# Block-causal attention and experts in one kernel: in the late turns, the scores of pair n on both sides of the sums of values of pair n-1

## The chip, the cores and the metric

The kernel runs on one core of a Trainium2 chip. The metric is the device time of one execution in microseconds (us); 1096.31 us is the median of three runs before the change. The engines named below are the tensor engine (PE, matmuls), the vector engine (DVE), the scalar engine (ACT), GpSimd (POOL) and the queue engine (SP). Each works through its own instructions in the order in which they were written into the program; semaphores tie the engines together. Matmuls write into PSUM, which the kernel uses as eight banks of 128 x 512 float32 (the tags `w0` to `w3`, `acc0` to `acc2` and `h`).

## The reference

Attention over 8 batches and 8 heads, 576 positions of 64 dimensions, masked in blocks of 64, and then two matmuls with a gate over all 4608 rows:

```python
scores = q @ k.T / 8                       # per batch and head, 576 x 576
mask = (pos[:, None] // 64) >= (pos[None, :] // 64)
attn = softmax(where(mask, scores, -1e9))
x = attn @ v                               # heads side by side: 4608 x 512
h = x @ w_in                               # 512 -> 2048
out = (h / (1 + exp(-1.702 * h))) @ w_out  # 2048 -> 512
```

All is float32. The kernel gets near-float32 products by splitting operands into a high and a low part (`high`, `low`; `xh`, `xl`; `wih`, `wil`; `gh`, `gl`) and adding three products.

## The kernel before

Two heads make a pair; there are 32 pairs, n = 0 to 31, and the program has 33 turns, one a pair and a last one for what is left over. Turns 0 to 7 are early turns, in which the weights of the experts are unpacked beside the attention. From turn 8 on the experts' matmuls run between the pieces of attention; turns 9 to 31 are the late turns of which this document speaks. Each turn is a row of slots (`ORDER`, `START`, `HANDOVER`, `FIRST_LATE`); after each slot `advance` writes as much of the experts' work as a schedule asks for. In turns from 9 on it always stops right behind the `hp` matmuls of a chunk (`state["gate"]`), so attention on PE always follows an `hp` matmul.

**Attention of a pair.** The 576 queries of a pair are cut into five rows: row 0 has 64 queries, rows 1 to 4 have 128, and row i needs 64(2i+1) keys, so 64, 192, 320, 448 and 576. For each row and head:

- scores: three matmuls on PE into a bank (`score_into`, from `high` and `low`);
- the score operation on DVE: mask, scale and running minimum of the bank in one instruction, with a small read-out instruction behind it (`weigh`, L439);
- exp with its sum on ACT (L446);
- normalising (`normalise`): two small instructions on DVE and a multiplication, on POOL for rows 0 to 3 and on DVE for row 4;
- transposes of the weights on DVE into `tw` (`turn`, L474 and L479), after which 16 DMAs on SP's queue bring them to `pw`; both are parts of the tile `turned`;
- the sums of values (`av`): 60 matmul instructions on PE from `pw` and the values `vp` into two banks, o0 and o, which ACT then copies to `xr` (L557, L558).

Before that, `prep_late` transposes q and k of a pair on DVE (L323), casts them to `high` on ACT (L324) and makes `low` on POOL.

**Banks.** In the experts' time three banks (w0, w1, w2) go round for attention, one more is lent by the experts (`lent_bank`: the spare one of two that hold `hp`), and the others hold `acc` and `hp`. The sums of a late turn take 320 columns of o0 and 256 of o. Row 4 has 576 keys and does not fit a bank: its first 384 go to two other banks, its last 192 lie beside the sums, in o0 for the first head and in o for the second (`beside` in `av`).

**A late turn before.** Slot 0 scores rows 3, 0, 2 and 1 of pair n in four banks, one stretch on PE. N and T normalise and transpose them. Slot V (`av(n-1)`) sums the values of pair n-1 and then scores row 4 of pair n; behind it come the preparation of pair n+1 (`prep`), row 4's normalising and transposing, and the DMAs to `pw`.

**Experts.** A tile is 384 rows. Per tile there are 16 chunks: 12 `hp` matmuls of 384 columns, then the gate: tanh on ACT (L673), a product on DVE (L674, tile g), a cast to `gh` on ACT (L682), the rest `gl` on POOL (L88). The nine `acc` matmuls of 512 columns of a chunk follow one chunk later. The gate's instructions have a high priority, by which a scheduler sets them among DVE's and ACT's other work; PE's matmuls keep the order of the code.

Of the kernel before, what the change touches and what calls it, by code (L numbers as in the profile page):

```python
# [25 lines left out]
ORDER = (  # L26
# [3 lines left out]
)  # L30
# [11 lines left out]
def attention_moe_kernel(  # L42
# [33 lines left out]
    def early(n):  # L76

        return n < 2 * HP
# [270 lines left out]
    def prep(n):  # L349

        if not parts_of(n):
            qk[n] = room("e0" if n % 2 else "qk", [P, 2, S], F32, "qk")
            for x in range(2):
                nc.vector.transpose(out=qk[n][:, x], in_=raw[n][:, x].rearrange("p c d -> p (c d)"))
        else:
            prep_late(n)
        raw.pop(n)
        m = follower(n)
        if m is not None:
            load(m)  # L360

    stats = {}
# [1 line left out]
    def score(n, banks):  # L364

        turns["late"] = not early(n)
        if n not in stats:
            mx = d2.tile([P, NCH + 1, 2], F32, tag="mx", name="mx")
            sm = d2.tile([P, NCH, 2], F32, tag="sm", name="sm")
            stats[n] = (mx, sm)  # L370
        todo = []
        taken = 0
        for chunks in banks:

            part = []
            for lo, hi in ((0, 512),) if width(chunks[0]) <= 512 else ((0, 256), (256, S)):
                ss = []
                for _ in range(2):
                    taken += 1
                    ss.append(lent_bank() if taken == 1 and turns["late"] else bank())  # L380
                c = 0
                for i in chunks:
                    a, z = qrange(i)
                    w = min(hi, width(i)) - lo
                    score_into(n, a, [x[:, c : c + w] for x in ss], lo, lo + w)
                    part += [(i, hd, lo, lo + w, ss[hd][0 : z - a, c : c + w]) for hd in range(2)]
                    c += w
            todo.append(sorted(part, key=lambda x: (chunks[::-1].index(x[0]), x[2])))
        settle(n, banks, todo)

    def settle(n, banks, todo):
        for chunks, part in zip(banks, todo):
            e = {}
            for i, hd, lo, hi, s in part:
                if i not in e:
                    e[i] = es[i] if early(n) else weights_of(n, i)
                weigh(n, i, hd, lo, hi, s, e[i])
            if early(n):
                for i in chunks[::-1]:
                    if n == 2 * HP - 1 and i == NCH - 1:  # L400
                        with tc.high_priority(offset=300):
                            normalise(n, i, e[i])
                    else:
                        normalise(n, i, e[i])
            else:
                weighed.extend((n, i, e[i]) for i in chunks[::-1])
            if 4 in chunks and not early(n):
                if n + 1 < NPAIR and n != 2 * HP:
                    prep(n + 1)
                normalise_all()  # L410
                turn_all()

    weighed = []
    shared = {}

    def weights_of(n, i):
        if i > 2:
# [5 lines left out]
    def normalise_all():  # L423
        for x in weighed:
            normalise(*x)

    def turn_all():
        for x in weighed:
            turn(*x)
        weighed.clear()  # L430

    def weigh(n, i, hd, lo, hi, s, e):
# [6 lines left out]
        nc.vector.tensor_tensor_reduce(  # L439
            out=e[0:m, hd, lo:hi], in0=s, in1=mk,  # L440
            op0=ALU.add, op1=ALU.min, scale=-0.125,
            scalar=3e38 if lo == 0 else mx[0:m, NCH, hd : hd + 1],
            accum_out=mx[0:m, i, hd : hd + 1] if hi == w else mx[0:m, NCH, hd : hd + 1],
        )
        if hi == w:
            nc.scalar.activation(  # L446
                out=e[0:m, hd], in_=e[0:m, hd], func=AF.Exp, scale=-1.0,
                bias=mx[0:m, i, hd : hd + 1], accum_out=sm[0:m, i, hd : hd + 1],
            )

    def normalise(n, i, e):
# [6 lines left out]
        if not early(n) and i == NCH - 1:  # L458
# [12 lines left out]
    def turn(n, i, e):  # L471

        for hd in range(2 if i else 0):
            nc.vector.transpose(  # L474
                out=tw[:, :, SLOT[i] : SLOT[i] + i, hd].rearrange("p b j c -> p j b c"),
                in_=e[:, hd, 0 : i * P],
            )
        r = slice(BLK, P) if i else slice(0, BLK)
        nc.vector.transpose(  # L479
            out=tw[r, 0:2, 9 + max(i, 1)].rearrange("p b h c -> p h b c"), in_=e[r, :, i * P : width(i)]  # L480
        )
        if i == NCH - 1:
            for kb in range(4):
                for qb in range(4):
                    ns = 10 if kb > 1 else NS if qb > 1 else 11
                    nc.sync.dma_start(
                        out=pw[kb * 32 : kb * 32 + 32, qb, 0:ns], in_=tw[qb * 32 : qb * 32 + 32, kb, 0:ns]
                    )

    def flip(n, chunks):  # L490

# [23 lines left out]
                in_=src[:, x : x + 2 * len(part), a : a + 2],  # L515
            )

    def av(n):

        b, h = divmod(n, HP)  # L520
        before_av(n)
        if turns["late"]:
            o0, o = bank(), bank()
            cut = BLK + 2 * P
        else:
            o, o0 = bank(), bank()
            cut = BLK

        def place(q0):
            return (o0, q0) if q0 < cut else (o, q0 - cut)  # L530

        todo = []
        for i in range(1, NCH):
# [3 lines left out]
        todo.append((*place(0), BLK, 0, pw[:, 0:2, 10]))  # L537

        ends = [[x for x, y in enumerate(todo) if y[0] is bk] for bk in (o0, o)]
        for x, (bk, c, nn, j, w) in enumerate(todo):  # L540
            for hd in range(2):
                mm(
                    out=bk[hd * D : hd * D + D, c : c + nn].rearrange("d (a c) -> d a c", c=32),
                    lhsT=values(n)[:, hd, j], rhs=w[:, :, hd],
                    start=any(x == y[0] for y in ends), stop=any(x == y[-1] for y in ends),
                )
        m = n + 1
        rest = []
        if turns["late"] and m < NPAIR:
# [6 lines left out]
        c0 = (b % 2) * S  # L556
        nc.scalar.copy(out=xr[:, h, c0 : c0 + cut], in_=o0[:, 0:cut])  # L557
        nc.scalar.copy(out=xr[:, h, c0 + cut : c0 + S], in_=o[:, 0 : S - cut])  # L558
        nxt = follower(n)
        if nxt is not None:  # L560
            load_v(nxt)
        if rest:
            settle(m, [[4]], [sorted(rest, key=lambda x: x[2])])

    def follower(n):

# [1 line left out]
        return None if m is None or m >= NPAIR else m  # L568

    def order(n):  # L570
        return {HP: START, 2 * HP: HANDOVER, 2 * HP + 1: FIRST_LATE}.get(n, ORDER[phase(n)]).split()

    def step(n):

# [3 lines left out]
        def item(x):  # L578
            if x == "V":
                return (lambda: av(n - 1)) if n else None  # L580
            if x in ("N", "T"):
                return normalise_all if x == "N" else turn_all
            if x == "L":
                return (lambda: prep(n + 1)) if n + 1 < NPAIR else None
# [150 lines left out]
    for n in range(NPAIR + 1):  # L735
        items = step(n)
        for sl, fn in enumerate(items):
            if fn is not None:
                fn()
            if order(n)[sl] == "V":  # L740
# [35 lines left out]
```

## Time and profile before

| what | us |
| --- | --- |
| three runs | 1095.48, 1096.31, 1097.78 |
| the profiled execution | 1096.38 |
| its span, first to last instruction | 1094.6 |
| PE busy in the span | 1057.5 |
| PE busy in the 100 us from 500 on | 99.94 |
| one late turn, first sums to first sums (573.44 to 604.67) | 31.2 |

The page names the engines' busy time and the costliest groups; the timeline gives start, duration, engine, line and tiles of every group of like instructions (x60 is 60 in a row). A line of a helper, such as L114 for all matmuls, stands for many places, so the tiles tell what is meant: `bank<-high` are scores, `bank<-turned,vp` sums of values, `hp<-` the experts' first matmuls, `acc<-` their second. Matmuls are pipelined, so the distance from start to start counts, not the duration shown.

### The profile page before, as it was taken

How to read it: one execution, taken by the hardware profiler on the slowest of the kernel's cores; microseconds unless marked ns; L12 is line 12 of the kernel's file. 1: busy time of each engine (PE TensorE's matmuls, PEld its weight loads, DVE VectorE, ACT ScalarE, POOL GpSimd, SP SyncE). 2: the span in 40 equal slices, each digit the busy share in tenths (PEclk: the TensorE clock that was granted, in tenths of full speed). 3: DMA queues.
4: the chain of work that ended last, by engine and by line, in shares of the span. 5: the costliest groups of instructions: out<-in, count | busy, mean ns of one | idle time of the engine just before them, and what ended most of it. 6: DMA issues, size and time to landing. Idle time of an engine off the chain costs nothing. (4 is left out here: it accounts for less than half of the span.)

```text
span 1094.6 us, 20705 instructions
## 1 busy us (share of the span) xinstructions
PE 1057.5 (97%) x7236; PEld 924.4 (84%) x7236; DVE 599.0 (55%) x1856; ACT 521.2 (48%) x1367; POOL 478.7 (44%) x601
## 2 busy tenths in 40 slices
PE   6869999999999999999999999999999999999998
PEld 3657777888889888899888888998888888999987
DVE  6786786845654656655655665655556655211111
ACT  5866776533534544534444543443544443322322
POOL 4666565634444444444444443443444343222222
PEclk8979999999999999999999999999999999999999
DMA  8734523333333443332434343333444322200000
GB/s 180 204 92 157 148 64 81 93 70 78 96 83 77 111 93 75 83 83 67 106 82 88 85 107 61 80 89 75 106 98 88 66 80 47 55 30 1 30 1 30
DMA packets 219369, 91.30 MB, mean 83 GB/s; under 512 B 197760, under 2 KB 197760, under 8 KB 219264
## 3 DMA queue, kind: packets, MB, share of 16 engines
q1 hardware_dynamic: 209344, 79.94, 32.3%
q10 hardware_dynamic: 9920, 10.03, 2.6%
q8 instruction: 57, 0.93, 0.4%
q14 instruction: 48, 0.39, 0.1%
HBM read 45.09 MB, written 9.44 MB: 50 GB/s over the span
## 5 line engine op out<-in xcount | busy, mean ns | idle before, releaser
L88 POOL TENSOR_TENSOR gl<-g,gh 128x384 fp32r<-128x384 f32 x192 | 195.6, 1019 | 447.1 <-ACT gh L682 428.4
L674 DVE SCALAR_TENSOR_TENSOR g<-g,hp 128x384 f32<-128x384 f32 x192 | 104.9, 546 | 354.7 <-ACT g L673 354.6
L114 PE MATMUL hp<-xh,wih 128*128 128x384 f32 x768 | 260.4, 339 | 2.9 <-DVE g L674 2.2
L114 PE MATMUL hp<-xh,wil 128*128 128x384 f32 x768 | 257.9, 336 | 0.0
L114 PE MATMUL hp<-xl,wih 128*128 128x384 f32 x768 | 253.8, 337 | 0.1
L114 PE MATMUL acc<-woh,gh 128*128 128x512 f32 x576 | 232.5, 404 | 0.8 <-ACT gh L682 0.7
L114 PE MATMUL acc<-wol,gh 128*128 128x512 f32 x576 | 227.3, 395 | 0.0
L673 ACT ACTIVATE g<-hp 128x384 f32<-128x384 f32 x192 | 93.7, 488 | 241.8 <-PE hp L114 207.2
L682 ACT CAST gh<-g 128x384 fp32r<-128x384 f32 x192 | 98.5, 513 | 169.4 <-DVE g L674 169.3
L114 PE MATMUL acc<-woh,gl 128*128 128x512 f32 x576 | 170.8, 394 | 1.4 <-POOL gl L88 1.4
L114 PEld LDWEIGHTS hp<-xh,wih 128*128 128x128 f32 x768 | 144.3, 188 | 16.0 <-issue 3.3
L114 PEld LDWEIGHTS hp<-xh,wil 128*128 128x128 f32 x768 | 144.2, 188 | 7.8
L114 PEld LDWEIGHTS hp<-xl,wih 128*128 128x128 f32 x768 | 143.6, 188 | 0.9 <-DVE xl L88 0.8
L446 ACT ACTIVATE e<-e,mx 64x64 f32<-64x64 f32 (+4 forms) x240 | 132.3, 554 | 20.0 <-DVE mx L439 20.0
L114 PEld LDWEIGHTS acc<-woh,gl 128*128 128x128 f32 x576 | 107.3, 188 | 28.1 <-POOL gl L88 4.5
L114 PEld LDWEIGHTS acc<-woh,gh 128*128 128x128 f32 x576 | 107.9, 187 | 25.1 <-ACT gh L682 1.8
L465 POOL TENSOR_TENSOR e<-e,sm 64x64 f32<-64x64 f32 (+1 forms) x192 | 112.8, 613 | 35.3 <-DVE sm L460 22.1
L114 PEld LDWEIGHTS acc<-wol,gh 128*128 128x128 f32 x576 | 108.3, 188 | 17.0 <-issue 0.4
L455 DVE TENSOR_SCALAR sm<-sm 128x2 f32<-128x2 f32 (+1 forms) x160 | 65.2, 408 | 60.4 <-ACT e L446 54.2
L439 DVE CUSTOM_DVE_ANT_0 e<-bank,mask 64x64 f32<-64x64 f32 (+4 forms) x240 | 93.2, 438 | 7.8 <-PE bank L114 7.1
L114 PEld LDWEIGHTS bank<-turned,vp 128*64 128x64 f32 x1800 | 85.4, 137 | 10.0 <-issue 7.0
L114 PE MATMUL bank<-turned,vp 128*64 128x128 f32 (+1 forms) x1800 | 89.6, 257 | 1.9 <-ACT turned L500 1.6
(62 smaller groups left out, 1199.5 us busy)
## 6 DMA issues: line engine op xcount, KB each, us to landing
turned<-turned SPq DMA_DIRECT2D x192, 80.0 KB, 2.1
turned<-turned SPq DMA_DIRECT2D x96, 112.0 KB, 2.3
raw<-in_q_dram SPq DMA_DIRECT2D x128, 72.0 KB, 2.4
out_dram<-osb ACTq DMA_DIRECT2D x36, 256.0 KB, 2.5
raw<-in_k_dram SPq DMA_DIRECT2D x120, 72.0 KB, 2.3
turned<-turned SPq DMA_DIRECT2D x96, 88.0 KB, 2.1
words<-in_moe_w_in_dram SPq DMA_DIRECT2D x16, 512.0 KB, 6.1
vp<-in_v_dram SPq DMA_DIRECT2D x60, 128.0 KB, 2.5
```

What stands on the lines that cost most here:

```text
L88: eng.tensor_tensor(out=out, in0=in0, in1=in1, op=ALU.subtract)
L114: return tc.keep_in_program_order(nc.tensor.matmul(**kw))
L439: nc.vector.tensor_tensor_reduce(out=e[0:m, hd, lo:hi], in0=s, in1=mk, op0=ALU.add, op1=ALU.min, scale=-0.125, scalar=3e38 if lo == 0 else ...
L446: nc.scalar.activation(out=e[0:m, hd], in_=e[0:m, hd], func=AF.Exp, scale=-1.0, bias=mx[0:m, i, hd : hd + 1], accum_out=sm[0:m, i, hd : hd ...
L455: x = nc.vector.tensor_scalar(out=c, in0=c, scalar1=1e-9, scalar2=2.0, op0=ALU.add, op1=ALU.mult)
L465: nc.gpsimd.tensor_tensor(out=x, in0=x, in1=sc.to_broadcast([m, width(i)]), op=ALU.mult)
L673: nc.scalar.activation(out=g, in_=hp[:, 0:tt], func=AF.Tanh, scale=1.702)
L674: nc.vector.scalar_tensor_tensor(out=g, in0=g, scalar=1.0, in1=hp[:, 0:tt], op0=ALU.add, op1=ALU.mult)
L682: nc.scalar.copy(out=gh, in_=g)
```

## The change

In turns 9 to 31 the two stretches of attention become one, slot M, on PE in this order: rows 0 and 3 of pair n; the last 192 keys of row 4, in o0 and o; the sums of values of pair n-1, in the order of rows 1, 2, 0 (bank o0), 3, 4 (bank o); the first 384 keys of row 4, in the banks that rows 0 and 3 had; rows 2 and 1, in the banks o0 and o. The score operations of row 4 take the two pieces in the reverse order. Turn 32 has the sums alone.

```diff
 ORDER = (
...
-    "3+0/2+1 - N - T - - V - - - - -",
+    "- - L - - M N4 N30 T4 N21 T -",
 )
...
-HANDOVER = "B C - 3+0/2+1 - - N - T - V - L - - -"
-FIRST_LATE = "3+0/2+1 - - N - - T - - V - - -"
+HANDOVER = "B C - 0+3/2+1 - - N - T - V - L - - -"
...
+    def score_row(n, chunks, ss):
+
+        c, part = 0, []
+        for i in chunks:
+            a, z = qrange(i)
+            w = width(i)
+            score_into(n, a, [x[:, c : c + w] for x in ss], 0, w)
+            part.append((i, [x[0 : z - a, c : c + w] for x in ss]))
+            c += w
+        for i, cols in part:
+            e = weights_of(n, i)
+            for hd in range(2):
+                weigh(n, i, hd, 0, width(i), cols[hd], e, True, True)
+            weighed.append((n, i, e))
+
+    def score_last(n, ss, lo, hi, e, first):
+
+        a, z = qrange(4)
+        score_into(n, a, ss, lo, hi)
+        for hd in range(2):
+            weigh(n, 4, hd, lo, hi, ss[hd][0 : z - a], e, first, not first)
+
+    def merged(n):
+
+        before_av(n - 1)
+        cut = LATE_CUT
+        now = n < NPAIR
+        if now:
+            new_stats(n)
+            score_row(n, (0, 3), [lent_bank(), bank()])
+        o0, o = bank(), bank()
+        if now:
+            e = weights_of(n, 4)
+            beside = [o0[:, cut : cut + S - K4], o[:, S - cut : S - cut + S - K4]]
+            score_last(n, beside, K4, S, e, True)
+        sums(n - 1, o0, o, cut, (1, 2, 0, 3, 4))
+        keep_sums(n - 1, o0, o, cut)
+        if now:
+            own = [x[:, 0:K4] for x in (lent_bank(), bank())]
+            score_last(n, own, 0, K4, e, False)
+            weighed.append((n, 4, e))
+            score_row(n, (2, 1), [bank(), bank()])
```

Beside that:

- Pair n is prepared in its own turn, three slots ahead of M (L), and not in the turn before; only pair 9 still is, in turn 8.
- The weights of row 4 of a late pair lie in the tile that q and k were loaded to (`raw`), so the load of the next pair follows row 4's transposes (T4); the 16 DMAs to `pw` (`send`) follow the last transposes of the turn (T).
- The transposes of a turn keep the order of the code on DVE, and so do fewer of the small normalising instructions.
- Turn 8 scores rows 0 and 3 in the order 0, 3.
- In the last chunk of the last tile the `acc` matmuls with `gh` of the first two thirds of the rows come before those with `gl`:

```diff
             if fc < NFC - 1:
...
                 todo.sort(key=lambda x: (fc == 0 and x[0] == 2, x[1] is g_lo))
+            elif t == NT - 1:
+                todo.sort(key=lambda x: (x[0] == 2, x[1] is g_lo))
```

More of the change, by code (lines that the diff above doesn't have):

```diff
@@ L358, in prep @@
         m = follower(n)
-        if m is not None:
+        if m is not None and n <= 2 * HP:
             load(m)
@@ L416, in weights_of @@
     def weights_of(n, i):
+        if i == 4 and parts_of(n):
+            return d2.tile([P, 2, S], F32, tag="raw", name="e", bufs=1)
         if i > 2:
@@ L421, in weights_of, with normalise_all, turn_all, weigh @@
         return shared[n][:, :, BLK * i * i : BLK * (i + 1) * (i + 1)]
-    def normalise_all():
+    def normalise_all(chunks=range(NCH)):
         for x in weighed:
-            normalise(*x)
-    def turn_all():
-        for x in weighed:
+            if x[1] in chunks:
+                normalise(*x)
+    def turn_all(chunks=range(NCH)):
+        for x in [y for y in weighed if y[1] in chunks]:
             turn(*x)
-        weighed.clear()
-    def weigh(n, i, hd, lo, hi, s, e):
+            weighed.remove(x)
+    def weigh(n, i, hd, lo, hi, s, e, first, final):
         mx, sm = stats[n]
@@ L457, in normalise @@
         )
-        if not early(n) and i == NCH - 1:
+        if n == 2 * HP and i == NCH - 1:
             tc.keep_in_program_order(x)
@@ L477, in turn, with send @@
             )
+            if n > 2 * HP:
+                tc.keep_in_program_order(x)
         r = slice(BLK, P) if i else slice(0, BLK)
-        nc.vector.transpose(
+        x = nc.vector.transpose(
             out=tw[r, 0:2, 9 + max(i, 1)].rearrange("p b h c -> p h b c"), in_=e[r, :, i * P : width(i)]
         )
[L482 to L488, printed above, removed]
+        if n > 2 * HP:
+            tc.keep_in_program_order(x)
+    def send():
+        for kb in range(4):
+            for qb in range(4):
+                ns = 10 if kb > 1 else NS if qb > 1 else 11
+                nc.sync.dma_start(
+                    out=pw[kb * 32 : kb * 32 + 32, qb, 0:ns], in_=tw[qb * 32 : qb * 32 + 32, kb, 0:ns]
+                )
     def flip(n, chunks):
@@ L516, in flip, with new_stats, sums @@
             )
[L518 to L527, printed above, removed]
+    def new_stats(n):
+        mx = d2.tile([P, NCH + 1, 2], F32, tag="mx", name="mx")
+        sm = d2.tile([P, NCH, 2], F32, tag="sm", name="sm")
+        stats[n] = (mx, sm)
+    def sums(n, o0, o, cut, by):
         def place(q0):
@@ L532, in av @@
         todo = []
-        for i in range(1, NCH):
+        for i in by:
+            if i == 0:
+                todo.append((*place(0), BLK, 0, pw[:, 0:2, 10]))
+                continue
             bk, c = place((i - 1) * P + BLK)
@@ L546, in av, with keep_sums @@
                 )
+    def keep_sums(n, o0, o, cut):
+        b, h = divmod(n, HP)
+        c0 = (b % 2) * S
+        nc.scalar.copy(out=xr[:, h, c0 : c0 + cut], in_=o0[:, 0:cut])
+        nc.scalar.copy(out=xr[:, h, c0 + cut : c0 + S], in_=o[:, 0 : S - cut])
+        nxt = follower(n)
+        if nxt is not None:
+            load_v(nxt)
+    LATE_CUT = BLK + 2 * P
+    def av(n):
+        before_av(n)
+        if turns["late"]:
+            o0, o = bank(), bank()
+            cut = LATE_CUT
+        else:
+            o, o0 = bank(), bank()
+            cut = BLK
+        sums(n, o0, o, cut, (1, 2, 3, 4, 0))
         m = n + 1
         rest = []
-        if turns["late"] and m < NPAIR:
+        if turns["late"]:
             own = [lent_bank(), bank()]
@@ L555, in av @@
                 rest += [(4, hd, lo, hi, ss[hd][0 : z - a]) for hd in range(2)]
[L556 to L561, printed above, removed]
+        keep_sums(n, o0, o, cut)
         if rest:
             settle(m, [[4]], [sorted(rest, key=lambda x: x[2])])
+    def score_row(n, chunks, ss):
[18 more added lines that the diff above has]
+        before_av(n - 1)
+        cut = LATE_CUT
+        now = n < NPAIR
+        if now:
+            new_stats(n)
+            score_row(n, (0, 3), [lent_bank(), bank()])
+        o0, o = bank(), bank()
+        if now:
[9 more added lines that the diff above has]
+            score_row(n, (2, 1), [bank(), bank()])
     def follower(n):
@@ L570, in order @@
     def order(n):
[L571 removed]
+        return {HP: START, 2 * HP: HANDOVER}.get(n, ORDER[phase(n)]).split()
     def step(n):
@@ L580, in item @@
                 return (lambda: av(n - 1)) if n else None
-            if x in ("N", "T"):
-                return normalise_all if x == "N" else turn_all
+            if x == "M":
+                return lambda: merged(n)
+            if x == "T4":
+                return lambda: (turn_all([4]), load(n + 1) if n + 1 < NPAIR else None)
+            if x == "T":
+                return lambda: (turn_all(), send() if now and n > 2 * HP else None)
+            if x[0] == "N":
+                return lambda: normalise_all([int(z) for z in x[1:]] or range(NCH))
             if x == "L":
-                return (lambda: prep(n + 1)) if n + 1 < NPAIR else None
+                m = n + 1 if n <= 2 * HP else n
+                return (lambda: prep(m)) if m < NPAIR and m not in high and m not in qk else None
             if x in ("a", "B", "C"):
@@ L739, in attention_moe_kernel @@
                 fn()
-            if order(n)[sl] == "V":
+            if order(n)[sl] in ("V", "M"):
                 heads_done = 2 * n
```

17 lines of the change are left out of this document (6 added, 11 removed).

## The prediction

> **What bounds the kernel now.** I read the page first, then the busy time by stretch, the waits of the tensor engine (PE), its timeline over one late turn, and the vector engine's (DVE) over the same turn. The page gives the span and what PE does in it:
>
> ```profile
> span 1094.6 us, 20705 instructions
> PE 1057.5 (97%) x7236; PEld 924.4 (84%) x7236; DVE 599.0 (55%) x1856; ACT 521.2 (48%) x1367; POOL 478.7 (44%) x601
> ```
>
> The profiled execution took 1096.38 us, 1.8 more than its span and 0.07 above the median of the three timed runs, so sums made on it carry over to the median. A tenth of the span from the late turns (PE busy and its instructions first, then the other engines, the granted clock, DMA), and the longest of PE's waits from 250 us to the end (total, times, longest):
>
> ```profile
> 500.00:600.00 100.00, 99.94 (x699) 89.74 (x698) 55.59 (x178) 44.91 (x118) 45.32 (x59) 1.00 0.37 83
> ```
>
> ```profile
> PE acc L114 <- POOL gl L88: 1.4, 5, 0.4
> ```
>
> So in the late turns PE is fed without a pause, at full clock. A time can shrink there only if the stream on PE gets shorter, and each microsecond for which PE is made to wait is added to the end, since nothing later has slack to give it back. The stream of one turn, PE alone:
>
> ```profile
> 573.17 0.34 PE L114 MATMUL hp<-xl,wih 128*128 128x384 f32 x1
> 573.44 2.98 PE L114 MATMUL bank<-turned,vp 128*64 128x128 f32 x60
> 576.35 0.44 PE L114 MATMUL bank<-high 64*128 64x384 f32 x2
> ...
> 576.98 0.25 PE L114 MATMUL bank<-high 64*128 64x192 f32 x2
> ...
> 577.38 0.50 PE L114 MATMUL acc<-woh,gh 128*128 128x512 f32 x1
> 577.72 0.40 PE L114 MATMUL acc<-wol,gh 128*128 128x512 f32 x1
> 577.96 0.39 PE L114 MATMUL acc<-woh,gh 128*128 128x512 f32 x1
> ...
> 585.67 0.34 PE L114 MATMUL hp<-xl,wih 128*128 128x384 f32 x1
> 585.94 0.47 PE L114 MATMUL bank<-high 64*128 64x448 f32 x2
> ...
> 586.80 0.39 PE L114 MATMUL bank<-high 64*128 64x320 f32 x2
> ...
> 587.33 0.25 PE L114 MATMUL bank<-high 64*128 64x192 f32 x2
> ...
> 587.73 0.50 PE L114 MATMUL acc<-woh,gh 128*128 128x512 f32 x1
> ```
>
> Attention breaks into the experts' matmuls twice a turn: at 573.44 the sums of values with row 4 of the scores behind them, at 585.94 rows 3, 0, 2 and 1. Each break has its price at the edges: an hp matmul streams for 0.17 us, so the first break could begin at 573.34 and begins 0.10 later; the first expert matmul after a break takes 0.34 us (577.38 to 577.72) where the next takes 0.24. The starts, not the durations, are to be read, since matmuls overlap.
>
> **What PE saves.** Now one stretch takes the place of the two. On PE, at the first break of a turn, before (names as in the code: turned is the transposed weights, vp the values, high and low the split queries and keys):
>
> ```order
> L114 MATMUL hp<-xl,wih 128x384
> L114 MATMUL bank<-turned,vp 64x128 x2
> L114 MATMUL bank<-turned,vp 64x64 x2
> L114 MATMUL bank<-turned,vp 64x128 x4
> L114 MATMUL bank<-turned,vp 64x64 x2
> L114 MATMUL bank<-turned,vp 64x128 x6
> L114 MATMUL bank<-turned,vp 64x64 x2
> L114 MATMUL bank<-turned,vp 64x128 x8
> L114 MATMUL bank<-turned,vp 64x64 x4
> L114 MATMUL bank<-high 128x384 x2
> ```
>
> and the one stretch of the changed kernel, to its first sums:
>
> ```order
> L113 MATMUL hp<-xl,wih 128x384
> L113 MATMUL bank<-high 64x64 x2
> L113 MATMUL bank<-high,low 64x64 x2
> L113 MATMUL bank<-low,high 64x64 x2
> L113 MATMUL bank<-high 128x448 x2
> L113 MATMUL bank<-high,low 128x448 x2
> L113 MATMUL bank<-low,high 128x448 x2
> L113 MATMUL bank<-high 128x192 x2
> L113 MATMUL bank<-high,low 128x192 x2
> L113 MATMUL bank<-low,high 128x192 x2
> L113 MATMUL bank<-turned,vp 64x128 x2
> ```
>
> Rows 0 and 3 and the last 192 keys of row 4 moved ahead of the sums; the 384 keys of row 4 and rows 2 and 1 stand behind them. The matmuls are the same. Before: 573.34 to 577.38 is 4.04, 585.84 to 587.73 is 1.89, together 5.93. After, from the same rows: entry 0.10; rows 0, 3 and the 192 keys 1.26 (585.94 to 587.73 is 1.79, less 0.53 for row 2 from 586.80 to 587.33); sums 2.91; 384 keys 0.63; rows 2 and 1 0.93; together 5.83, and one slow first expert matmul less (0.10). If nothing waits, a turn saves 0.2 us. Score operations of the second part of row 4 are counted x48 in the trace, two heads each, so 24 pairs, of which the first is scored in the old way still: 23 turns are merged. That part is worth 23 x 0.2 = 4.6 us at most.
>
> **What the stretch waits for.** The banks o0 and o that take the sums now hold the last 192 keys of row 4 first (score_last with beside, before sums). The sums of a bank can begin only when DVE has read these scores out of it, even though the columns differ: the program keeps bank users apart, as this row of DVE's waits (200 us to the end) shows, where the same score operation had to wait for ACT's copy of other columns of o0:
>
> ```profile
> DVE e L439 <- ACT xr L557: 4.8, 22, 1.1
> ```
>
> By the Trainium skill (PSUM — Partial Sum Buffer, PSUM bank collisions raise a hardware error) two engines on one bank and the same quarter of partitions must be kept apart whether or not their columns overlap; by it the wait cannot be dropped, and only without it would the 4.6 us remain as a gain.
>
> On DVE the operation that frees o0 stands behind others. Before, behind a turn's sums (T of the last turn's weights, the two transposes of the next pair's q and k, then row 4):
>
> ```order
> L323 STREAM_TRANSPOSE qt<-raw 128x576
> L323 STREAM_TRANSPOSE raw<-raw 128x576
> L439 ISA e,mx<-bank,mask 128x384
> L439 ISA mx 128x1
> L439 ISA e,mx<-bank,mask 128x384
> L439 ISA mx 128x1
> L439 ISA e,mx<-bank,mask,mx 128x192
> L439 ISA mx 128x1
> ```
>
> now, from the gate of the expert chunk (g) that ends right before the stretch:
>
> ```order
> L746 SCALAR_TENSOR_TENSOR g<-g,hp 128x384 x2
> L438 ISA e,mx<-bank,mask 64x64
> L438 ISA mx 64x1
> L438 ISA e,mx<-bank,mask 128x448
> L438 ISA mx 128x1
> L438 ISA e,mx<-bank,mask 64x64
> L438 ISA mx 64x1
> L438 ISA e,mx<-bank,mask 128x448
> L438 ISA mx 128x1
> L438 ISA e,mx<-bank,mask 128x192
> L438 ISA mx 128x1
> ```
>
> Before, PE had gone on to the experts when DVE came to the 192 keys. Now this operation is sixth in the row, behind the gate (the second of the two g) and the four of rows 0 and 3, and PE can do nothing until it is done. DVE's rows, in time:
>
> ```profile
> 574.12 0.56 DVE L674 SCALAR_TENSOR_TENSOR g<-g,hp 128x384 f32<-128x384 f32 x1 [2.90 <-ACT g L673]
> ...
> 578.06 0.52 DVE L439 CUSTOM_DVE_ANT_0 e<-bank,mask 128x384 f32<-128x384 f32 x1
> ...
> 579.25 0.42 DVE L439 CUSTOM_DVE_ANT_0 e<-bank,mask,mx 128x192 f32<-128x192 f32 x1 [0.17 <-ACT xr L557]
> 579.59 0.08 DVE L439 DVE_READ_ACCUMULATOR2_ANT mx<- 128x1 f32 x1
> ...
> 584.42 0.52 DVE L674 SCALAR_TENSOR_TENSOR g<-g,hp 128x384 f32<-128x384 f32 x1
> ...
> 587.13 0.55 DVE L674 SCALAR_TENSOR_TENSOR g<-g,hp 128x384 f32<-128x384 f32 x1 [1.85 <-ACT g L673]
> 587.60 0.21 DVE L439 CUSTOM_DVE_ANT_0 e<-bank,mask 64x64 f32<-64x64 f32 x1
> ...
> 588.98 0.07 DVE L439 DVE_READ_ACCUMULATOR2_ANT mx<- 128x1 f32 x1
> ```
>
> Count from the start of the last hp matmul. The gate begins 0.95 later (573.17 to 574.12; the tanh on ACT lies between), the first score operation 0.47 after it (587.13 to 587.60), the four of rows 0 and 3 take 1.38 (587.60 to 588.98), the 192 keys 0.42 with their read-out (579.25 to 579.59, and 0.08). DVE frees o0 at 3.22. PE gets there at 0.17 + 0.10 + 1.26 = 1.53. PE waits 1.69 us in each of the 23 turns. The second head's 192 keys, behind one small operation that waits for an exp, are read at about 3.9 (an estimate: one exp's read-out, that small operation and 0.42 more), while PE still has o0's 40 percent of the sums (12 of 30, 1.16 us) to do until 4.4: no second wait. The 384 keys need the banks of rows 0 and 3, free since 2.8. Rows 2 and 1 need ACT's two copies of the sums; the last can begin when the sums end and has 0.63 of row 4 to hide behind, which is just about its length: 0, at worst 0.2.
>
> **What comes behind it.** The stretch ends about 7.75 after that hp matmul (3.22 + 2.91 + 0.63 + 0.93). On DVE the first gate after it now stands behind more: before, row 4's normalising and transposes alone,
>
> ```order
> L455 TENSOR_SCALAR sm<-sm 128x2
> L460 RECIPROCAL sm<-sm 128x2
> L467 TENSOR_SCALAR e<-e,sm 128x576 x2
> L474 STREAM_TRANSPOSE turned<-e 128x4x4x32 x2
> L674 SCALAR_TENSOR_TENSOR g<-g,hp 128x384
> ```
>
> now also rows 2 and 1 and the transposes of row 3:
>
> ```order
> L466 TENSOR_SCALAR e<-e,sm 128x576
> L473 STREAM_TRANSPOSE turned<-e 128x4x4x32 x2
> L480 STREAM_TRANSPOSE turned<-e 64x2x2x32
> L454 TENSOR_SCALAR sm<-sm 128x2 x2
> L459 RECIPROCAL sm<-sm 128x2 x2
> L480 STREAM_TRANSPOSE turned<-e 64x2x2x32
> L473 STREAM_TRANSPOSE turned<-e 128x3x4x32 x2
> L746 SCALAR_TENSOR_TENSOR g<-g,hp 128x384
> ```
>
> The transposes' mean, and one of the two casts of the next pair on ACT that stood before row 4's exps:
>
> ```profile
> L474 DVE STREAM_TRANSPOSE turned<-e 128x512 f32<-128x512 f32 (+3 forms) x186 | 79.1, 481 | 0.4 <-DMA turned<-turned 0.4
> ```
>
> ```profile
> 579.38 0.69 ACT L324 CAST high<-qt 128x576 fp32r<-128x576 f32 x1
> ```
>
> Before, 6.36 us passed from row 4's first operation to that gate (578.06 to 584.42). Now add four score operations (1.38) and two transposes (0.96), and take off the two casts, which are now done earlier and no longer delay row 4's exps (up to 1.4): 7.3 to 8.7. They count from about 6.9, when PE has the first 384 keys done, so the gate starts at 14.2 to 15.6 and the cast behind it is out some 1.1 later (twice a gate's 0.55), at 15.3 to 16.7. PE needs it after 8.46 of expert work (577.38 to 585.84), at 16.2. So between nothing and 0.5; I take 0.1.
>
> The rest counts as nothing. Preparing the next pair (L) moves to the start of its own turn, three places ahead of its use, with two expert chunks between; if that cover went, its chain of transposes, casts and subtracts would show as a wait on low. The load of q and k and the sends of the weights now go out later on SP, but have several places of the turn left before their use. In the last tile the new order of the second matmuls changes PE's end, but the three copies out follow each other on ACT from the first one, which starts no sooner.
>
> Sum per turn: 1.69 - 0.2 + 0.1 = 1.6; 23 x 1.6 = 36.8; 1096.4 + 36.8 = 1133.2, say 1133.
>
> **Rivals.** *The merge pays* (0.06): DVE is done with the 192 keys by the time PE is there, or the wait is short, and 0.2 a turn remains: 1096.4 - 4.6 = 1092. It decides at 1.53 us behind the last hp matmul; for it speaks only that PE's two edges are real, against it that the gate's 0.95 and 0.47 alone take 1.42. *No wait to speak of and no gain* (0.03): the two cancel, at a wait of 0.2: 1096. *The gate becomes the bound as well* (0.16): the list on DVE runs longer than summed, PE waits 0.8 a second time: 23 x 2.3 = 53, 1149. *The clock falls* (0.10): early in the run, stretches of 3.41 us (PE busy in them, clock) show
>
> ```profile
> 13.24:16.65 3.41, 1.53 (x14) 1.00 0.78 126
> 16.65:20.07 3.42, 3.01 (x17) 0.50 0.64 129
> ```
>
> a stretch with 1.53 of 3.41 busy is followed by one at half clock. A wait of 1.69 leaves 1.72 busy, just above that. If half of the turns lost 1.7 us in this way, 20 more would come: 1153. The Trainium skill (TensorE: Matmul & The Clock Gate, Part 1) has the clock fall after an idle window of some 3.4 us; by it 1.69 us of waiting is too short, and the 1133 stays.
>
> **How the numbers follow.** My case has 0.65. Its own bounds are a wait 0.5 shorter with no gate wait (1.0 a turn, 1119) and a gate wait of 0.5 more (2.1 a turn, 1145). The range takes in the gate rival and stops short of the clock: 1119 to 1150. The two clauses left out above and below hold 0.19. About 0.2% can be told from no change here. Faster by more than that 0.06, within it 0.03, slower 0.91.
>
> **What would show it.** Right: PE's waits gain a row bank <- DVE mx of about 1.7 us, some 23 times, ahead of the first sums of each stretch; the stretch is 7.5 to 8 us long; the granted clock stays 1.00. The gate term shows as acc <- ACT gh. Wrong: no such row, or the DVE's 192-key operation ahead of the gate in time; PE's waits on low, on ACT's xr copies or on the sends (turned) would each mean a cover that I counted and that is gone; a clock below 1.00 after 250 us means the fourth rival.

## The result, and the profile after

The change made the kernel slower: 1155.49 us (median of five runs, 1154.69 to 1159.48) against 1097.78 us for the kernel before in the same measurement (1095.48 to 1098.45). The ratio is 1.0546, with a 95% interval from 1.0532 to 1.0561. The forecast was 1133, with a range of 1119 to 1150; the time came out above the range. The sign was right, the size was not: 36.8 us were forecast, 57.7 came. The profiled executions read below took 1157.04 and 1096.38 us; their spans are 60.5 us apart, and the sums are made for these 60.5.

The page of the changed kernel, beside the one of before:

```profile
span 1155.1 us, 20680 instructions
PE 1070.7 (93%) x7236; PEld 936.8 (81%) x7236; DVE 568.8 (49%) x1856; ACT 529.3 (46%) x1367; POOL 477.3 (41%) x601
```

PE runs the same 7236 matmuls. Its idle time went from 37.1 us (1094.6 less 1057.5) to 84.4 (1155.1 less 1070.7), which is 47.3 more. Its busy time also grew, by 13.2 us, although no matmul was added. So there are two things to find: waits, and matmuls that take longer. The waits of PE from 200 us to the end (total, times, longest):

```profile
PE bank L113 <- DVE mx L438: 31.8, 20, 1.6
PE acc L113 <- ACT osb L711: 9.3, 8, 1.7
PE bank L113 <- DVE sm L454: 5.4, 2, 2.8
PE acc L113 <- POOL gl L87: 3.5, 5, 1.3
PE bank L113 <- DVE sm L459: 2.5, 1, 2.5
PE acc L113 <- ACT gh L754: 0.6, 1, 0.6
```

They sum to 53.1 us; in the kernel before, such waits came to 4.3 us from 200 us on. The first row is the wait that was forecast, in 20 of the 23 turns. The second row had no place in the forecast. The rows on DVE sm are three stretches in which the sums began 2.5 to 2.8 us late, for another reason.

One stretch of the changed kernel as PE runs it (start, duration):

```profile
528.57 0.34 PE L113 MATMUL hp<-xl,wih 128*128 128x384 f32 x1
528.84 0.24 PE L113 MATMUL bank<-high 64*64 64x64 f32 x2
...
529.93 0.28 PE L113 MATMUL bank<-low,high 64*128 64x192 f32 x2
531.79 2.98 PE L113 MATMUL bank<-turned,vp 128*64 128x128 f32 x60 [1.59 <-DVE mx L438]
...
536.22 0.50 PE L113 MATMUL acc<-woh,gh 128*128 128x512 f32 x1
```

and DVE in the same stretch:

```profile
529.53 0.56 DVE L746 SCALAR_TENSOR_TENSOR g<-g,hp 128x384 f32<-128x384 f32 x1 [3.64 <-ACT g L745]
530.00 0.21 DVE L438 CUSTOM_DVE_ANT_0 e<-bank,mask 64x64 f32<-64x64 f32 x1
...
531.38 0.34 DVE L438 CUSTOM_DVE_ANT_0 e<-bank,mask 128x192 f32<-128x192 f32 x1
531.66 0.08 DVE L438 DVE_READ_ACCUMULATOR2_ANT mx<- 128x1 f32 x1
```

PE has written its last score of row 4 at about 530.2 and stands until DVE has read row 4 out of o0, at 531.74. From the last hp matmul to the first expert matmul (528.74 to 536.22) the stretch is 7.48 us long, where the forecast said 7.5 to 8.

The rest of the loss is in the clock. The profile has the granted clock in windows of 3.41 us. Two of them, each with the next one behind it, and a third alone (PE busy in the window and its instructions, granted clock, DMA share, GB/s):

```profile
357.27:360.68 3.41, 1.82 (x29) 1.00 0.00 0
360.68:364.09 3.41, 3.41 (x46) 0.50 0.00 0
459.67:463.08 3.41, 1.83 (x32) 1.00 0.01 2
463.08:466.50 3.42, 3.42 (x64) 1.00 0.10 23
527.95:531.36 3.41, 2.25 (x24) 1.00 0.02 5
```

```profile
360.26 4.63 PE L113 MATMUL bank<-turned,vp 128*64 128x128 f32 x60 [1.59 <-DVE mx L438]
```

The first time the wait of 1.59 us falls wholly into a window (1.82 of 3.41 us busy), and the next window runs at half clock: the sums take 4.63 us instead of 2.98. At 527.95 it lies across the end of a window (2.25 busy), and nothing follows. But a wait wholly inside a window does not always do it: at 459.67, and also at 801.00 (1.82 busy) and 732.73 (1.85), the next window is at full clock, and so it is behind 667.88, with only 1.54 busy. In the four stretches in which the clock fell behind this wait, the wait began 1.4 to 1.8 us into the window; at 459.67, 801.00 and 732.73 it began 0.8 to 1.2 us into it. Whether that is what decides was not tried.

The half clock came in 5 of the 23 stretches: 4 of the 20 with that wait, and one of the three with the longer wait for the sends. Over the whole run the mean granted clock is 0.981, against 0.991 before. The clock withheld 0.019 x 1155.1 = 21.9 us after and 0.009 x 1094.6 = 9.9 before: 12.0 us more, some 8 of them in these five stretches (1.5 to 1.65 each, as 4.63 less 2.98). The rest lies in the first 100 us (0.90 and 0.83 in its halves, against 0.93 and 0.86), ahead of the merged turns. The merge is not needed for it to differ: in the first 250 us the clock is 0.95 here, 0.96 before, and 0.96 again in two merged kernels below with the same early turns (the one without the output's DMAs and the one a slot earlier). Why it varies there stays open.

Together: 53.1 - 4.3 of waits and 12.0 of clock are 60.8, for a span that grew by 60.5. Nothing is left over for what the merge saves.

Two more views belong to the rows that were not forecast. ACT behind the stretch that ends a tile of the output:

```profile
300.29 0.44 ACT L445 ACTIVATE e<-e,mx 128x192 f32<-128x192 f32 x1
...
300.73 1.04 ACT L711 COPY osb<-acc 128x512 f32<-128x512 f32 x2
...
304.12 0.58 ACT L711 COPY osb<-acc 128x512 f32<-128x512 f32 x1
```

```profile
301.34 0.50 PE L113 MATMUL acc<-woh,gh 128*128 128x512 f32 x1 [1.17 <-ACT osb L711]
...
304.75 0.50 PE L113 MATMUL acc<-woh,gh 128*128 128x512 f32 x1 [1.74 <-ACT osb L711]
```

The copies that empty a finished tile's acc banks stand behind the exps of rows 2 and 1, which now end right behind the stretch. The next tile's first acc matmul waits for the first pair of copies, and a later one for the third, which stands behind the next tanh and cast on ACT.

And the sends of the weights on SP:

```profile
376.96 17.53 SPq L491 DMA_DIRECT2D turned<-turned  x16
```

```profile
SPq L491 <- DMA out_dram<-osb: 7.7, 2, 6.7
```

```profile
396.50 2.98 PE L113 MATMUL bank<-turned,vp 128*64 128x128 f32 x60 [2.76 <-DVE sm L454]
```

Sixteen sends usually take 10 to 12 us; these took 17.5, because SP stood 6.7 us for a transfer of the output. PE was ready for the sums at 393.74 and could have begun at some 395.3, as elsewhere; the last send left SP at 394.49 and the sums began at 396.50, though the row names DVE. The same stoppage was there before, and did no harm:

```profile
616.02 18.48 SPq L486 DMA_DIRECT2D turned<-turned  x16
```

```profile
636.53 2.99 PE L114 MATMUL bank<-turned,vp 128*64 128x128 f32 x60
```

There, sums came 20.5 us after the first send (636.53 less 616.02), so 18.5 us of sending fitted. Now PE is there after 16.8 us (393.74 less 376.96), so it does not.

### The profile page after: what moved, and what is told of

Read it like the earlier page. It is cut to its first block, busy times and chain, and to the rows that moved or that the text cites. A ratio compares the mean times of both kernels' runs of the same rounds, so it can differ in the third digit from the quotient of the medians.

```text
span 1155.1 us, 20680 instructions
## 1 busy us (share of the span) xinstructions
PE 1070.7 (93%) x7236; PEld 936.8 (81%) x7236; DVE 568.8 (49%) x1856; ACT 529.3 (46%) x1367; POOL 477.3 (41%) x601
## 5 line engine op out<-in xcount | busy, mean ns | idle before, releaser
L464 POOL TENSOR_TENSOR e<-e,sm 64x64 f32<-64x64 f32 (+3 forms) x192 | 113.2, 618 | 217.8 <-DVE sm L459 192.5
L113 PE MATMUL bank<-turned,vp 128*64 128x128 f32 (+1 forms) x1800 | 99.3, 273 | 41.3 <-DVE mx L438 31.8
L113 PEld LDWEIGHTS bank<-turned,vp 128*64 128x64 f32 x1800 | 95.2, 149 | 47.5 <-DVE mx L438 35.2
L473 DVE STREAM_TRANSPOSE turned<-e 128x256 f32<-128x256 f32 (+2 forms) x192 | 85.8, 483 | 2.5 <-POOL e L464 1.1
L438 DVE CUSTOM_DVE_ANT_0 e<-bank,mask 128x192 f32<-128x192 f32 (+4 forms) x240 | 84.7, 402 | 2.3 <-PE bank L113 2.2
```

The lines of the kernel that those rows point to most:

```text
L113: return tc.keep_in_program_order(nc.tensor.matmul(**kw))
L438: nc.vector.tensor_tensor_reduce(out=e[0:m, hd, lo:hi], in0=s, in1=mk, op0=ALU.add, op1=ALU.min, scale=-0.125, scalar=3e38 if first else m ...
L464: nc.gpsimd.tensor_tensor(out=x, in0=x, in1=sc.to_broadcast([m, width(i)]), op=ALU.mult)
L473: x = nc.vector.transpose(out=tw[:, :, SLOT[i] : SLOT[i] + i, hd].rearrange("p b j c -> p j b c"), in_=e[:, hd, 0 : i * P],)
```

## The experiments

Each ratio is to the kernel before, timed beside it on the same chip (1096.6 to 1097.4 us). The changed kernel itself stands at 1.0546 (1.0532 to 1.0561).

| kernel | us | ratio | 95% interval | clock |
|---|---|---|---|---|
| row 4 first | 1123.28 | 1.0233 | 1.0217 to 1.0248 | 0.986 |
| a score operation twice | 1179.02 | 1.0758 | 1.0721 to 1.0796 | 0.972 |
| stretch behind acc | 1235.19 | 1.1261 | 1.1233 to 1.1288 | 0.954 |
| row 4 first, behind acc | 1193.62 | 1.0875 | 1.0833 to 1.0917 | 0.974 |
| order of the last tile alone | 1096.38 | 0.9991 | 0.9981 to 1.0001 | 0.991 |
| copies earlier | 1161.19 | 1.0577 | 1.0549 to 1.0605 | 0.975 |
| row 4 first, copies earlier | 1132.10 | 1.0319 | 1.0301 to 1.0336 | 0.977 |
| row 4 first, copies and their DMAs earlier | 1118.89 | 1.0203 | 1.0181 to 1.0225 | 0.983 |
| row 4 first, output of all tiles but the last left out | 1105.14 | 1.0073 | 1.0057 to 1.0089 | 0.990 |
| row 4 first, one slot later | 1260.15 | 1.1488 | 1.1463 to 1.1512 | 0.925 |
| row 4 first, one slot earlier | 1256.73 | 1.1463 | 1.1437 to 1.1488 | 0.922 |
| row 4 first, preparation earlier | 1256.88 | 1.1466 | 1.1443 to 1.1489 | 0.922 |

**Row 4 first.** The theory: PE waits because DVE reads row 4 behind the four score operations of rows 0 and 3. Here the 192 keys of row 4 are scored ahead of rows 0 and 3, on PE and on DVE, so that o0 is free earlier. Nothing else changes.

```diff
-            score_row(n, (0, 3), [lent_bank(), bank()])
+            ss = [lent_bank(), bank()]
         o0, o = bank(), bank()
...
             score_last(n, beside, K4, S, e, True)
+            score_row(n, (0, 3), ss)
```

> The 192 keys of row 4 are scored ahead of rows 0 and 3, on PE and on DVE; all else as in the changed kernel. Theory (PE stands still until DVE has read row 4 out of o0, and the clock falls because of that standstill): DVE frees o0 at 0.95 + 0.47 + 0.42 = 1.84 us behind the last hp matmul instead of 3.2, PE is there at 1.5, so the wait falls from 1.59 to about 0.3 us in each of 23 turns (-30 us), and the five windows of half clock go (-8): about 1117 us. Rival (the cost sits in the new places of the preparation, the transposes and the sends, and the wait only shows where it collects): the wait moves to another row of PE's waits and the time stays within 10 us of 1155.

It took 1123.28, 32 us less than the changed kernel. Its waits on PE, 200 us to the end:

```profile
PE acc L113 <- ACT osb L712: 9.3, 8, 1.7
PE bank L113 <- DVE sm L459: 7.9, 3, 2.7
PE acc L113 <- POOL gl L87: 3.5, 5, 1.3
PE bank L113 <- DVE mx L438: 3.3, 18, 0.2
```

The wait on row 4 went from 31.8 to 3.3 us, and an undisturbed stretch lasts 6.1 instead of 7.5. The clock no longer falls behind these stretches; it still falls behind two of the three late sends. The other rows stayed, to the tenth (the late sends, 5.4 and 2.5, now stand in one row of 7.9). So the wait is DVE's reading of row 4, and the copies (osb) and the late sends (under DVE sm) have other causes. 26 us of loss are left.

**A score operation twice.** The same wait made longer: in the changed kernel, row 3's score operation of one head is done twice, 0.55 us more ahead of row 4's.

```diff
+        if n > 2 * HP and i == 3 and hd == 0:
+            nc.vector.tensor_tensor_reduce(
...
+            )
```

> The changed kernel with the score operation of row 3 done twice for the first head, ahead of row 4's on DVE: 0.55 us more. Theory: every wait grows by 0.55 to 2.1 us (+12.5 us in 23 turns), and PE being idle for more of a window of 3.41 us, the half clock comes in more turns than 5 (each 1.65 us): 1168 to 1185 us. Rival (clock falls have nothing to do with the length of the wait): 5 windows as before, 1168 us. If the wait is not DVE's doing: 1155 us.

It took 1179.02, 23.5 us more than the changed kernel. The wait:

```profile
PE bank L113 <- DVE mx L438: 42.7, 20, 2.2
```

It grew by 0.55 us a time, 11 to 13 us over the turns. The other half of the loss is the clock: 13 of the 23 stretches now have a window at half clock instead of 5 (12 with this wait, one with a wait of 3.4 us for the sends), and the clock withheld 0.028 x 1177.0 = 33 us instead of 21.9. So here a longer wait cost about twice what it added.

**Stretch behind acc.** This asks whether the gate is what DVE is late with, as the forecast had it. The turn's stop moves behind the acc matmuls of the previous chunk, so that the stretch follows acc and the gate is over long before.

```diff
-                yield ("gate", fc)
                 if prev is not None:
                     yield from second(prev)
+                yield ("gate", fc)
```

> The stretch follows the acc matmuls of a chunk and no longer its hp matmuls, so the gate (tanh, product on DVE) is over when it begins; its own order is unchanged. If the gate ahead of the score operations is what PE waits for, the wait falls by about 1 us a turn, and the time to about 1130 us. If it is the four score operations of rows 0 and 3, which cannot begin before PE has scored row 3, the wait stays at about 1.5 us and the time within 10 us of 1155.

It took 1235.19. DVE ahead of one stretch's sums:

```profile
476.31 0.55 DVE L746 SCALAR_TENSOR_TENSOR g<-g,hp 128x384 f32<-128x384 f32 x1 [3.63 <-ACT g L745]
476.78 0.77 DVE L322 STREAM_TRANSPOSE raw<-raw 128x576 f32<-128x576 f32 x1
480.55 0.22 DVE L438 CUSTOM_DVE_ANT_0 e<-bank,mask 64x64 f32<-64x64 f32 x1 [3.00 <-PE bank L113]
...
481.94 0.35 DVE L438 CUSTOM_DVE_ANT_0 e<-bank,mask 128x192 f32<-128x192 f32 x1
```

```profile
PE bank L113 <- DVE mx L438: 28.3, 19, 1.5
PE acc L113 <- POOL gl L87: 17.3, 23, 1.3
PE bank L113 <- POOL low L87: 14.9, 22, 0.7
PE bank L113 <- ACT high L323: 12.5, 22, 0.8
```

The gate is out at 476.86, 3.7 us before the first score operation, and PE waits 1.5 us on row 4 all the same. So the gate is not needed for this wait. What holds DVE is that the four operations of rows 0 and 3 (480.55 to 481.94) can begin only when PE has scored row 3's keys, and that row 4's stands behind them. In the changed kernel the gate happens to end at just that moment (530.00, the first score operation's start). The new waits on high and low show a cover that is gone: the second transpose of the pair's q and k (476.78) now stands behind the last gate before the stretch, and cast and subtract follow in the open.

**Row 4 first, behind acc.** Both edits together.

> Both: the 192 keys first, and the stretch behind the acc matmuls. Theory: DVE reads row 4 as soon as it is scored, about 1.2 us into the stretch, and PE is there at 1.4: no wait, no fall of the clock, a stretch of 5.8 us. What is left over the kernel before are the waits within the experts' work (13.9 us more than before in the changed kernel) less the 4.6 us of the merge: 1105 to 1112 us. Rival (new places of the other work): above 1130 us.

It took 1193.62: 42 us less than the stretch behind acc, 70 us more than row 4 first alone. The wait on row 4 is gone there as well (2.4 us in all), and the waits on low (27.7 us, 22 times) and high (12.5) stand in the foreground. Row 4's place is worth 32 us in the one place of the stretch and 42 in the other. Behind acc the preparation is the largest part of the loss (40.2 us on low and high), beside gl (17.3 against 3.5), the sends (15.1 against 7.9) and the clock.

**The order of the last tile alone.** The kernel before with the new order of acc matmuls in the last chunk of the last tile.

```diff
             if fc < NFC - 1:
...
+            elif t == NT - 1:
+                todo.sort(key=lambda x: (x[0] == 2, x[1] is g_lo))
```

> The kernel before with the new order of the acc matmuls in the last chunk of the last tile alone. Theory (the first copy out sets the end and starts no sooner): within 0.1% of before. Rival (PE's wait of 0.5 us for gl comes off the end): 0.5 us faster.

It took 1096.38, a ratio of 0.9991 over five rounds (0.9981 to 1.0001): no difference clear of the noise, as counted. The rival, 0.5 us faster, is too small to be told from it.

**Copies earlier.** The next question is the 9.3 us on osb. The copies of a finished tile get a higher priority in the scheduler, in the changed kernel and in the one with row 4 first.

```diff
-                    nc.scalar.copy(out=osb, in_=acc[c])
+                    with tc.high_priority(offset=1000):
+                        nc.scalar.copy(out=osb, in_=acc[c])
```

> The changed kernel with the copies of finished output tiles given a high priority, so that on ACT the first two stand behind two of the stretch's exps less than before (at three tile ends; the third copy still waits for a free output buffer). Theory (the new waits acc <- ACT osb, 9.3 us in all, are copies queued behind the exps of the merged stretch): 1.2 us less at three tile ends, 1150 to 1153 us; the 23 waits on DVE stay. Rival (PE waits there for something else): 1155 us.

> Row 4's 192 keys first, and the copies earlier. Theory: 1123 less 3 to 5 us, 1118 to 1120. Rival: 1123.

Neither became faster. The one with row 4 first is slower, 1132.10 against 1123.28; for the changed kernel, 1161.19 against 1155.49, the two intervals overlap. The first two copies moved ahead of three of the exps, and their DMAs went out behind them, but the third copy came no earlier. In the one with row 4 first, ACT and PE:

```profile
295.10 1.05 ACT L713 COPY osb<-acc 128x512 f32<-128x512 f32 x2
295.69 0.34 ACTq L715 DMA_DIRECT2D out_dram<-osb  x1
...
299.69 0.51 ACT L756 CAST gh<-g 128x384 fp32r<-128x384 f32 x1 [1.74 <-DVE g L748]
300.11 0.58 ACT L713 COPY osb<-acc 128x512 f32<-128x512 f32 x1
```

```profile
300.74 0.50 PE L113 MATMUL acc<-woh,gh 128*128 128x512 f32 x1 [3.34 <-ACT osb L713]
```

A finished tile has three copies and two buffers, so the third copy needs the first one's buffer. The expectation of the next run puts its lateness down to DMAs that stayed behind the exps; the rows show another thing. The first DMA went out at 295.69 and such DMAs take some 2.1 us to land, so the buffer was free at about 297.8 (an estimate). But in the order that the scheduler gave ACT the third copy stands behind the next tanh and cast, and ACT stood 1.74 us for the gate's product from DVE ahead of that cast. Two waits of 1.2 and 1.7 us became one of 3.3, which also cost clock (0.977 against 0.986).

**Row 4 first, copies and their DMAs earlier.** Now the priority covers the copy and its dma_start.

> Row 4's 192 keys first, and both the copies of a finished output tile and their DMAs get the high priority. With the copies alone so raised the time rose by 9 us, because the DMAs stayed behind the exps and the third copy waited for the first DMA to free its buffer. Theory (that buffer is what the third copy waits for): the third copy comes earlier by the two exps of 192 keys, the single wait of 3.4 us at three tile ends shrinks to about 2, below what made the clock fall, and the time is 1117 to 1122 us. Rival (any copy put ahead of exps delays the rest as much as it gains): 1128 to 1133 us.

```profile
PE acc L113 <- ACT osb L714: 4.1, 5, 1.2
```

The third copy now stands ahead of the cast (copy at 297.80, cast at 298.27, at the same end of a tile). The waits on osb fell from 9.3 to 4.1 us, so ACT's order is their cause. The time went from 1123.28 to 1118.89, though the two intervals touch. It is the lowest time here of a merged kernel that writes its whole output, and still 2.03% (1.81 to 2.25) slower than before.

**Row 4 first, without the output's DMAs.** This takes away what SP waits for in the sends. The DMAs that write the output are left out for all tiles but the last; the copies stay.

```diff
-                    tc.keep_in_program_order(nc.scalar.dma_start(out=out[r : r + P, :], in_=osb))
+                    if t == NT - 1:
+                        tc.keep_in_program_order(nc.scalar.dma_start(out=out[r : r + P, :], in_=osb))
```

> Row 4's 192 keys first, and the DMAs of the output are left out except for the last tile's (the copies stay). Theory: three stretches of 8.5 to 10.2 us are long because SP's sends of the weights waited for an output DMA that shares a semaphore with them and had itself waited for ACT; without these DMAs all stretches take 6.1 us and the clock never falls (-10.6 us), and the third copy of a tile no longer waits for its buffer (-5 us): 1106 to 1112 us. Rival (sends late for want of time between a turn's transposes and the next sums, whatever the output does): the long stretches stay, 1117 to 1123 us.

It took 1105.14, 18 us less than row 4 first. The sends of the turn that was late there, and the waits that are left:

```profile
364.00 10.09 SPq L491 DMA_DIRECT2D turned<-turned  x16
```

```profile
PE bank L113 <- DVE mx L438: 4.1, 21, 0.5
PE acc L113 <- ACT osb L712: 3.5, 3, 1.2
```

No send takes longer than 11.5 us, no stretch waits for one, and the clock falls behind no merged stretch. The output's DMAs are what stops the sends. Of the 18 us, 7.9 are the rows on the sends (0.8 of them back in the row on mx), 5.8 the third copies (9.3 less 3.5), which now follow the first two at once; the rest is about what the clock gave back. The waits that remain (some 11.6 us with 4.0 on gl and gh, against 4.3 before) account for most of the 8 us that this kernel is slower than before.

**Other places in the turn.** The question was whether the waits for copies and the late sends come from where the ends of the tiles fall in the turn: the preparation (L), the stretch and all behind it move one slot later, or one earlier. In the third kernel the stretch is one slot earlier and L two, four slots ahead of the stretch, which should cover the preparation again. All with row 4 first; the last also with the copies and their DMAs earlier.

```diff
-    "- - L - - M N4 N30 T4 N21 T -",
+    "- - - L - - M N4 N30 T4 N21 T",
```

```diff
-    "- - L - - M N4 N30 T4 N21 T -",
+    "- L - - M N4 N30 T4 N21 T - -",
```

```diff
-    "- - L - - M N4 N30 T4 N21 T -",
+    "L - - - M N4 N30 T4 N21 T - -",
```

> Row 4's 192 keys first, and the preparation, the stretch and all behind it one slot (a twelfth of a turn) later. Theory (waits for copies and late sends come from where tile ends fall in the turn): another set of tile ends meets the stretch, and the waits acc <- ACT osb (9.3 us) and the long stretches (10.6 us with the clock) change by more than 5 us in sum, either way. Rival (they come with the merged stretch wherever it lies): 1119 to 1127 us.

> The same with the preparation, the stretch and all behind it one slot earlier. On ACT the copies of an output tile then stand behind the first tanh that follows the exps, and the tile ends meet the stretch elsewhere. Theory (the place of the tile ends): the waits for copies and the long stretches change by more than 5 us in sum; the preparation, two expert chunks ahead of the scores, may show as waits on high and low of some 0.5 us a turn. Rival: 1119 to 1127 us.

> The stretch one slot earlier as in the last, the preparation two slots earlier, at the start of the turn, and copies and DMAs raised. Theory: any waits of PE on high and low that the one-slot shift brought are covered again, and the time is the better of the shifted ones, 1105 to 1118 us. Rival (raw lands too late for it, or DVE's transposes of q and k then stand in the way of the last weights): waits on high and low stay, above 1123 us.

All three took 1257 to 1260 us, 133 us and more over row 4 first. One slot earlier, DVE ahead of a stretch and PE in it:

```profile
520.14 0.56 DVE L747 SCALAR_TENSOR_TENSOR g<-g,hp 128x384 f32<-128x384 f32 x1 [3.64 <-ACT g L746]
520.61 0.77 DVE L322 STREAM_TRANSPOSE raw<-raw 128x576 f32<-128x576 f32 x1
```

```profile
PE bank L113 <- ACT high L323: 58.4, 22, 2.9
PE bank L113 <- POOL low L87: 23.5, 22, 1.3
```

PE stands in 22 turns for the transpose, cast and subtract of the pair's q and k, because DVE does the second transpose behind the last gate before the stretch. One slot later has the same row (57.8 us, 22 times). L written earlier left it at 58.4: in the order on DVE that transpose stays behind the last gate. In the changed kernel's place two more gates stand between it and the stretch (transpose at 521.63, stretch at 528.84), and no wait on low or high is among PE's rows. So the preparation's cover exists in that place alone, of those tried. With waits of 2.6 and 1.2 us in one turn the clock also falls in nearly every turn, for two windows in most: 0.922, or 98 us withheld. The question about the ends of the tiles is not answered by these runs, since the lost cover outweighs it. Why the scheduler keeps the transpose behind that gate was not tried further.

## Why the prediction was wrong in size

**The wait on row 4: right.** Forecast 1.69 us in 23 turns, measured 1.59 in 20; in the other three it is hidden in a longer one. Row 4 first takes the wait away, a score operation twice lengthens it by what it adds. In the working of that step the gate was named as what stands ahead; the stretch behind acc shows that rows 0 and 3 alone do it. Gate and row 3's scores are ready at the same moment, so the number came out right with half of its reason, in part by luck.

**The merge's own gain: too large.** Forecast 0.2 us a turn. The stretch with row 4 first is 6.1 long with 0.2 of wait in it, so 5.9, against 5.93 for the two stretches and 0.1 for one slow expert matmul before: some 0.1 a turn at the stretch. In the whole turn none of it is left: from one turn's sums to the next's an ordinary turn takes 31.23 us before and 32.83 after, and 32.83 less the wait of 1.59 is 31.24. Where the 0.1 goes stays open. The growth of 1.6 is also the forecast's sum for a turn, but by luck: there it was a wait that was 0.1 too long, a gain that does not show, and a gate that does not show in such a turn.

**The gate behind the stretch: right on the average, not in its form.** 0.1 a turn was forecast, as waits on gh; the waits on gl and gh are 4.1 us in all, against 2.1 before. The only wait on gh (0.6) lies at 209.7, ahead of the first merged stretch. What is new are two waits of 1.28 us on gl, in 2 of the 23 turns, so the average is luck.

**"The load of q and k and the sends of the weights now go out later on SP, but have several places of the turn left before their use": failed.** The sends had 16.8 us, enough for the usual 10 to 12 and not for the 17.5 that they take when SP is stopped by a DMA of the output. The trace of before had the 18.48 us row; I did not set the longest duration against the time left. Three turns lost 2.5 to 2.8 us in place of 1.6, some 3 us more.

**"The rest counts as nothing": failed for ACT.** The copies of a finished tile were not in the list of what moves. The exps of rows 2 and 1 moved ahead of them, 9.3 us of waits in eight places; moving copies and DMAs ahead gave back 5.2 of them.

**The clock: the rival came true beside my case, not in its place.** It had a chance of 0.10, for half of the turns and 1.7 us each. It came in 5 of 23 stretches at 1.5 to 1.65 us each: about 8 us. The step that failed was to take 1.72 busy as "just above" the 1.53 of the early rows, and so as safe. A window with 1.82 busy is followed by one at half clock, while one with 1.54 is not, so the busy share of a window alone does not tell it. The Trainium skill (TensorE: Matmul & The Clock Gate, Part 1) has the clock fall after an idle window of some 3.4 us; the trace differs, with 1.59 us of idle in such a window, and the trace decides.

**The preparation's cover, the tail, the second head, rows 2 and 1: right.** No wait on low or high is among PE's rows, the order of the last tile makes no difference clear of the noise, and no second wait stands behind the first in the stretch.

What failed, then, are terms that the sum put at nothing: the copies on ACT (9.3 us), the late sends (3) and the clock (12, some 8 of it in the merged turns). The sum that would have met it: the 36.6 of the wait (1.59 x 23), plus 9.3 for the copies, 3 for the late sends, 12 for the clock (some 4 of them ahead of the merged turns), 2 for the gate, less 2 for other waits of the kernel before that are gone, and nothing for the merge. That is 61, for a span 60.5 longer.

## What to carry to other kernels

A bank that two engines share in one stretch ties the reader's whole queue to the writer: put the read that frees it first in that queue, and count what stands ahead of it by what can start, not only by what is queued. When a stretch moves, go through every queue that it passes, and set the longest duration in the trace against the time that is left, not the usual one. In a stream that is at full clock, price a wait of about half a clock window above its own length: some of these waits, not all, were followed by a window at half clock, and more of them at 2.1 us than at 1.59.

## What the runs showed of the hardware

- The granted clock of PE can halve for a window of 3.41 us behind a window in which PE was busy for 1.82 us, with an idle time of 1.59 us. It need not: behind windows with 1.54 and 1.83 us busy it stayed at full. What decides between them was not tried. Waits of 2.1 us did it in 12 of 20 stretches, waits of 1.59 in 4 of 20, waits of 0.2 in none.
- SP's sends stood for a transfer that ACT had issued, of other data, for 6.7 us. With those transfers left out, no wait of these sends on a transfer is left, and no sixteen of them took longer than 11.5. Why sends stand for a transfer of another engine is not shown here; a shared DMA semaphore was the guess.
